# An attention and gated-MLP kernel on one core: another order of the first loads

## The chip, the cores and the metric

The kernel runs on one core of one Trainium2 chip. The metric is the time of one execution on the device in microseconds (us); lower is better. Five engines work side by side, each with its own queue of instructions: TensorE (PE, with weight loads shown as PEld), VectorE (DVE), ScalarE (ACT), GpSimd (POOL) and SyncE (SP), whose queue mostly issues transfers (DMA).

## The reference

One input x of 2048 rows and 640 columns (bf16) is normalised by rows and goes into two branches, whose results are added to x:

```
xn  = (x - mean(x)) / sqrt(var(x) + 1e-5)
qkv = xn @ wqkv                        # wqkv: 640 x 1920; 32 heads of 20
logits[s, w] = q[s] . k[s - 2w] * 20**-0.5     # w = 0..7; -1e9 where s - 2w < 0
o   = sum_w softmax(logits)[s, w] * v[s - 2w]
A   = o @ wo                           # 640 x 640
B   = ((xn @ w_gate) * (xn @ w_up)) @ w_down   # 640 x 1536, 640 x 1536, 1536 x 640
out = x + A + B
```

## The kernel before, in words

**Tiles.** The 2048 rows are 16 row tiles of 128 (a load is 128 x 640 bf16, 160 KB) and 4 blocks of 512 rows. The 640 columns are 5 chunks of 128 (`NCH`). A weight matrix lies in SBUF as chunks of 128 of its rows; `wqkv_load(g, lo, hi)` (L517) loads rows of chunks lo to hi of Q (g = 0), K (1) or V (2), 160 KB for each chunk. `x_load(t)` (L511) loads row tile t.

**Stages.** In the first stage (`front(t)`, L566, one for each row tile) VectorE takes the statistics of the tile in two halves (L574) and joins them (L577), ScalarE takes the root (L584), VectorE the reciprocal (L591) and, for tiles 0 to 5, the normalised rows (L603 in two parts for tiles 0 and 1, L606 for 2 to 5); from tile 6 on ScalarE normalises (L609) and the root is taken for two tiles at once. TensorE transposes tiles 0 to 3 (L642) and VectorE or ScalarE copies them from PSUM (L653, L655, L662); later tiles are transposed by DMA (L675). TensorE then projects Q and K: for tiles 0 and 1 by `spread` (L730), in two parts, chunks 0 to 1 and chunks 2 to 4, as the transposed rows come; for all others and for V by `mms` (L698). ScalarE evicts the projections (L703). Ahead of the first transposes TensorE runs ten dummy matmuls of 512 columns (`warm`, L682) and three of 256 behind them.

The second stage multiplies Q with shifted K on VectorE (L881, L930), sums some products on GpSimd (L956, L967, L989) and the heads' columns on TensorE (L1013: the logits); softmax follows on VectorE and ScalarE. In the third, VectorE multiplies V by the weights (L1192), GpSimd adds pairs (L1197) and TensorE sums the rest in four batches (L1251). The MLP's matmuls (L1315) and the output's (L1416, L1467) fill TensorE throughout.

**What sets the order.** The kernel is planned when it is built. `Sched` holds a clock for every engine and for the data path; each task names what it reads and writes, a priority and its PSUM banks. `run` (L235) takes for each engine, among the tasks that could start within a short patience, the one of the best priority, and emits the one that starts earliest. What an instruction costs in the plan is `occ`; a transfer ends in the plan when its bytes would have passed, or at `land` where that is given. The result is a fixed order for each engine with semaphore waits for the true dependences, so `land` and `occ` alone issue nothing, but they set the order.

The first loads are written out by hand (L1521 to L1529) and all go through SP's queue; `loads` (L521) goes on with tiles 3 to 11, then V's weights, then the last four tiles as their slots come free. Tile 1 starts its statistics only after tile 0 is normalised, and tile 2 after tile 1 (`have("apply", ...)`, L614 to L618). An instruction that waits holds up all behind it on its engine.

Of the kernel before, what the change touches and what calls it, by code (L numbers as in the profile page):

```python
# [11 lines left out]
NCH = 5  # L12
# [343 lines left out]
def build_kernel(nc, A_x, A_wqkv, A_wo, B_x, B_w_gate, B_w_up, B_w_down, out):  # L356
# [25 lines left out]
    NXS = 12  # L382
# [78 lines left out]
    def mark(*k):  # L461
        done.add(k)
# [4 lines left out]
    def have(*k):  # L467
        return lambda: k in done

    def num(n, *k):  # L470
        return lambda: count.get(k, 0) >= n
# [4 lines left out]
    def dma(o, i, r=(), w=(), name="", eng="sp", group=None, land=None):  # L476
        n = mybir.dt.size(o.dtype)
        for s in o.shape:
            n *= s
        return op(eng, lambda e: e.dma_start(o, i), r=r, w=w, dma=True, name=name, nbytes=n, group=group, land=land)  # L480
# [27 lines left out]
    def xslot(t):  # L508
        return t + 4 if t < 8 else t - 8

    def x_load(t, eng="sp", land=None):  # L511
        dma(XST[:, xslot(t), :], xhbm[t * TS:(t + 1) * TS, :], w=[XST[:, xslot(t), :]], name=f"xld{t}", eng=eng, land=land)
        mark("x", t)
# [3 lines left out]
    def wqkv_load(g, lo=0, hi=NCH, eng="sp", land=None):  # L517
        dst = WQKV[:, WPOS[g], lo:hi, :]
        dma(dst, wqkv_src[:, lo:hi, g * D:(g + 1) * D], w=[dst], name=f"ld_wqkv{g}_{lo}", eng=eng, land=land)

    def loads():  # L521
        def t(f, *a):
            return Task("sp", lambda: f(*a), prio=0)

        for t_ in range(3, NXS):
            yield t(x_load, t_)
        yield t(wqkv_load, 2)
        for t_ in range(NXS, NT):
            yield have("apply", t_ - NXS)
            yield t(x_load, t_)  # L530

        def w(T, src):
            dma(T[:], src.rearrange("(c p) n -> p c n", p=128), w=[T[:]], name="ld_w")

        def pads():
            z = ZERO[:, 0:PAD].unsqueeze(1).to_broadcast([128, NCH, PAD])
            dma(vscr[:, 0:PAD].rearrange("(c p) s -> p c s", p=128), z, r=[ZERO[:, 0:PAD]], w=[("vscr", "pad")], name="vpad")

        yield have("xnt", NT - 1)
        yield t(w, WG, B_w_gate)  # L540
        yield t(pads)
        yield t(w, WU, B_w_up)

        def copy_x():
            a, b = ohbm[0:3 * JB, :], xhbm[0:3 * JB, :]
            o, i = a.rearrange("(p r) n -> p (r n)", p=128), b.rearrange("(p r) n -> p (r n)", p=128)
            op("sp", lambda e: e.dma_start(o, i), w=[("outx",)], dma=True, name="outx", nbytes=2e6)

        yield num(2, "lg")
        yield t(copy_x)  # L550
# [15 lines left out]
    def front(t):  # L566
        x, st = XST[:, xslot(t), :], STATS[:, t, 0:12]
        xs, mv = XNS[:, t % NXN, :], MV[:, t, 0:2]
        sd, rstd, nmr = SD[:, t, 0:1], SD[:, t, 1:2], SD[:, t, 2:3]
# [9 lines left out]
        ts = next((g for g in GROUPS if t in g), (t,))  # L579
        t0, t1 = ts[0], ts[-1] + 1  # L580

        def sqrt():
            o, i = SD[:, t0:t1, 0:1], MV[:, t0:t1, 1:2]
            op("act", lambda e: e.activation(o, i, ACT.Sqrt, bias=EPSC[:, 0:1]), r=[("mv", k) for k in ts] + [EPSC[:]],  # L584
               w=[("sd", k) for k in ts], name=f"sd{t}", occ=0.25)
            for k in ts:
                mark("sd", k)

# [37 lines left out]
        if t == ts[-1]:  # L626
            yield Task("act", sqrt, r=[("mv", t)], prio=p - 1)
            yield Task("dve", recip, r=[("sd", t)], prio=p)
# [892 lines left out]
    x_load(0, land=3.2)  # L1521
    tch = A_wqkv.rearrange("(c k p) n -> k c p n", k=16, c=NCH)[:, :, 0, 0:32]
    stores.append(dma(TCH[0:16], tch, w=[TCH[0:16]], name="touch", eng="act"))
    wqkv_load(0, 0, 3, land=5.3)
    x_load(1, land=5.7)
    wqkv_load(0, 3, NCH, land=7.0)
    wqkv_load(1, 0, 3, land=8.5)
    x_load(2, land=9.0)
    wqkv_load(1, 3, NCH, land=10.0)  # L1529
    K.t["act"] = 2.1  # L1530
    warm(10, JB)

    def misc():
# [6 lines left out]
        yield Task("act", lambda: op("act", preload, name="exp_preload", occ=1.3), prio=6)  # L1540

    K.spawn(loads())
    for t in range(NT):
        K.spawn(front(t))
# [19 lines left out]
def bass_parallel_sum__sliding_local_dilated__glu_gated_bilinear__prompt_kernel(  # L1564
    nc, A_x, A_wqkv, A_wo, B_x, B_w_gate, B_w_up, B_w_down, out
):
    build_kernel(nc, A_x, A_wqkv, A_wo, B_x, B_w_gate, B_w_up, B_w_down, out)
# [28 lines left out]
```

## Time and profile before

| what | value |
|---|---|
| median of 3 runs | 265.47 us (265.27, 265.48, 265.47) |
| the profiled execution, its own time | 265.01 us |
| its span, first to last instruction | 263.3 us, 4080 instructions |
| granted clock of TensorE | 1.00 |
| VectorE busy | 218.9 us, 83% |
| ScalarE busy | 112.8 us, 43% |
| GpSimd busy | 160.6 us, 61% |

The profile is of one execution. Its pages give the busy time of each engine, the chain of work that ended last (followed back from the last instruction, at each step to what released it), groups of instructions by line, and for transfers the time from issue to landing. A line in a timeline is: start, length, engine, line, operation, tile written <- tile read, count, and in brackets the idle time before it with what ended it. Lengths of matmuls are modelled and overlap, so the pace of a row of matmuls is read from the starts of the first and of what follows. Transfers are named by the tile that they fill: XST is a row tile of x, WQKV weight rows.

### The profile page before, as it was taken

The numbers are of one execution on the slowest core, as the hardware profiler recorded it, in microseconds if no ns is written. First come the engines' busy times: TensorE is split into PE (matmuls) and PEld (weight loads), VectorE is DVE, ScalarE is ACT, GpSimd is POOL, SyncE is SP. The second block draws the span as 40 slices with busy tenths as digits, with TensorE's granted clock in tenths as the row PEclk, the third lists the DMA queues.
The fourth block names the chain that finished last, engine by engine and source line by source line (L and its number), as shares of the span: only waits on it lengthen the run. The fifth ranks groups of instructions, "written<-read, shape, count | busy, mean of one in ns | idle before, by whom it ended". The sixth has DMA issues, their size and how long they took to land.

```text
span 263.3 us, 4080 instructions
## 1 busy us (share of the span) xinstructions
PE 258.1 (98%) x1566; PEld 135.9 (52%) x1587; DVE 218.9 (83%) x259; ACT 112.8 (43%) x198; POOL 160.6 (61%) x97
## 2 busy tenths in 40 slices
PE   7999999999999999999999999999999999999996
PEld 3996965444444444444444444444444444445675
DVE  4687899999998798778779999999999989994041
ACT  3559987556612221224258656521350144211300
POOL 3000000000599998899973576799989999999100
PEclk9999999999999999999999999999999999999999
DMA  6964699970479996470249424847779676721621
GB/s 212 373 218 81 121 104 366 416 281 12 122 133 186 217 229 129 88 142 1 62 129 309 88 47 109 169 113 171 177 174 208 149 162 137 110 55 37 94 62 50
DMA packets 47843, 39.78 MB, mean 151 GB/s; under 512 B 23856, under 2 KB 45488, under 8 KB 47792
## 3 DMA queue, kind: packets, MB, share of 16 engines
q1 hardware_dynamic: 44848, 33.29, 49.5%
q0 software_dynamic: 2736, 6.16, 13.6%
q8 instruction: 12, 0.20, 0.3%
q10 hardware_dynamic: 240, 0.07, 0.1%
q14 instruction: 7, 0.06, 0.1%
HBM read 25.07 MB, written 7.23 MB: 123 GB/s over the span
## 4 chain that ended last, share of the span: by engine, by line
PE 91%; ACT 6%; issue 1%; DMA 1%; DVE 1%
PE PS L1315 39%; PE PS L1416 21%; PE PS L698 17%; PE PS L1467 7%; ACT XNS L609 3%; PE PS L730 2%; PE PS L1013 2%; PE PS L1251 2%; DMA XST<-in_A_x_dram 1%; ACT QT L703 1%; PE PS L642 1%; ACT VST L703 1%; ACT KT L703 1%; ACT SD L584 0%; DVE STATS L574 0%
## 5 line engine op out<-in xcount | busy, mean ns | idle before, releaser
L1197 POOL TENSOR_TENSOR SV<-PV 128x1024 bf16<-128x1024 f32 x40 | 94.2, 2522 | 15.7 <-DVE HT L1362 3.6
L1192 DVE TENSOR_TENSOR PV<-VX,PS 128x1024 f32<-128x1024 bf16 (+1 forms) x54 | 90.9, 1729 | 2.3 <-POOL SV L1197 2.3
L698 PE MATMUL PS<-XNT,WQKV 128*128 128x512 bf16 (+2 forms) x384 | 60.0, 316 | 0.5 <-issue 0.3
L1315 PE MATMUL PS<-XNT,WU 128*128 128x512 bf16 x239 | 59.4, 379 | 0.2 <-issue 0.2
L1315 PE MATMUL PS<-XNT,WG 128*128 128x512 bf16 x231 | 57.7, 379 | 0.6 <-ACT LOG L1024 0.2
L698 PEld LDWEIGHTS PS<-XNT,WQKV 128*128 128x128 bf16 x390 | 37.8, 112 | 21.9 <-ACT LOG L1024 0.8
L930 DVE TENSOR_TENSOR PRF<-PS,KT 128x1024 f32<-128x1024 f32 x32 | 37.9, 1217 | 0.3 <-PE PS L698 0.3
L1315 PEld LDWEIGHTS PS<-XNT,WU 128*128 128x128 bf16 x240 | 23.4, 98 | 28.5 <-ACT OT L1260 0.4
L1315 PEld LDWEIGHTS PS<-XNT,WG 128*128 128x128 bf16 x240 | 23.4, 98 | 28.5 <-issue 0.4
L956 POOL TENSOR_TENSOR PRF<-PRF,PRF 128x1024 f32<-128x1024 f32 x8 | 22.0, 2751 | 20.6 <-DVE LOG L1073 20.6
L703 ACT ACTIVATE HT<-PS 128x512 bf16<-128x512 f32 x24 | 14.3, 597 | 34.5 <-PE PS L1315 34.5
L881 DVE TENSOR_TENSOR PRD<-QT,KT 128x2048 bf16<-128x2048 bf16 x24 | 27.3, 1223 | 0.0
L1416 PE MATMUL PS<-HT,WD 128*128 128x512 bf16 x117 | 27.2, 380 | 0.1
L1032 POOL MEMSET LOG<- 32x6 bf16 (+6 forms) x7 | 0.4, 95 | 43.7 <-ACT LOG L1024 43.7
L703 ACT ACTIVATE UX<-PS 128x512 bf16<-128x512 f32 x15 | 9.0, 597 | 40.6 <-PE PS L1416 40.6
L989 POOL TENSOR_TENSOR PRD<-PRF,PRF 128x1024 bf16<-128x1024 f32 x8 | 21.4, 2759 | 0.1
L967 POOL TENSOR_TENSOR PRF<-PRF,PRD 128x1024 f32<-128x1024 f32 x8 | 19.5, 2544 | 0.0
L1416 PEld LDWEIGHTS PS<-HT,WD 128*128 128x128 bf16 x120 | 11.7, 98 | 14.3 <-ACT OT L1260 0.4
L1416 PE MATMUL PS<-OT,WO 128*128 128x512 bf16 x75 | 18.6, 379 | 0.1
L1480 DVE TENSOR_TENSOR FB<-PS,XR 128x320 bf16<-128x320 f32 (+2 forms) x9 | 4.1, 455 | 17.4 <-PE PS L1467 16.9
L1324 DVE TENSOR_TENSOR HT<-HT,PS 128x512 bf16<-128x512 bf16 x18 | 12.3, 684 | 7.0 <-PE PS L1315 7.0
L574 DVE BATCH_NORM_STATS2 STATS<-XST 128x6 f32<-128x320 bf16 x32 | 14.0, 470 | 2.4 <-DMA XST<-in_A_x_dram 2.4
(76 smaller groups left out, 246.4 us busy)
## 6 DMA issues: line engine op xcount, KB each, us to landing
VX<-v_scratch SPq DMA_DIRECT2D x80, 130.0 KB, 3.0
PRF<-PRF POOLq DMA_DIRECT2D x8, 512.0 KB, 5.1
XST<-in_A_x_dram SPq DMA_DIRECT2D x16, 160.0 KB, 5.3
v_scratch<-VST SPq DMA_DIRECT2D x4, 640.0 KB, 6.3
WG<-in_B_w_gate_dram SPq DMA_DIRECT2D x1, 1920.0 KB, 9.8
WU<-in_B_w_up_dram SPq DMA_DIRECT2D x1, 1920.0 KB, 14.0
out_dram<-in_A_x_dram SPq DMA_DIRECT2D x1, 1920.0 KB, 20.0
WD<-in_B_w_down_dram SPq DMA_DIRECT2D x1, 1920.0 KB, 8.1
```

Source lines behind the costliest of these rows:

```text
L698: op("pe", (lambda o, l, x, c, first: lambda e: e.matmul(o, l, x, start=first, stop=(c == NCH - 1)))(o, l, x, c, first), r=[l, x], w=[o], ...
L703: X = op("act", (lambda o, i: lambda e: e.activation(o, i, ACT.Copy))(o, i), r=[i], w=[o], name=name, occ=0.12 + n * 0.9e-3)
L881: op("dve", lambda e: e.tensor_tensor(s[:], qb, kv, ALU.mult), r=[q, rk], w=[s[:]], name=f"prod{j}_{r}_{c}", occ=1.15, lock=True)
L930: X = op("dve", lambda e: e.tensor_tensor(o[:], qb, kv, ALU.mult), r=[q, rk, ("qev", j, c)], w=[o[:]], name=f"prow{j}_{r}_{c}_{q0}", occ=1.17)
L956: yield Task("pool", lambda: op("pool", lambda e: e.tensor_tensor(x, x, y, ALU.add), r=[x, y] + tokens(), w=[x], name=name, occ=2.36, lock ...
L967: yield Task("pool", lambda: op("pool", lambda e: e.tensor_tensor(x, x, z, ALU.add), r=[x, z] + tokens(), w=[x], name=name + "c", occ=2.36 ...
L989: yield Task("pool", lambda: op("pool", lambda e: e.tensor_tensor(o, a, y, ALU.add), r=[a, y] + tokens(), w=[o], name=f"qend{j}_{r}_{q0}", ...
L1192: last[0] = op("dve", lambda e: e.tensor_tensor(p, vw, a, ALU.mult), r=[vv] + rk, w=[p], name=f"pv{u}_{x}_{r0}", occ=0.09 + 1.1 * nr)
L1197: X = op("pool", lambda e: e.tensor_tensor(o, p[:, :, 0, :], p[:, :, 1, :], ALU.add), r=[p[:]] + tokens(), w=[o], name=f"pva{u}_{x}", occ= ...
L1315: op("pe", (lambda l, x, c: lambda e: e.matmul(PS[:, b, :], l, x, start=(c == 0), stop=(c == NCH - 1)))(l, x, c), r=[l, x], w=[PS[:, b, :] ...
L1416: op("pe", (lambda l, x, i: lambda e: e.matmul(PS[:, b, :], l, x, start=(i == 0), stop=(i == n - 1)))(l, x, i), r=[l, x], w=[PS[:, b, :]], ...
L1467: op("pe", (lambda l, x, i: lambda e: e.matmul(dst, l, x, start=(i == 0), stop=(i == n - 1)))(l, x, i), r=[l, x], w=[PS[:, b, :]], name=f" ...
```

## The change

The loads written out by hand get another order and one more transfer. Before: tile 0, Q chunks 0-2, tile 1, Q 3-4, K 0-2, tile 2, K 3-4, and tile 3 from `loads`. After: tile 0, Q chunk 0, tile 1, Q 1-2, Q 3-4, tile 2, K 0-2, tile 3, K 3-4. The landing times given to the plan change with it, and so does the plan's cost of the root. Bytes, tiles and the work on every engine are the same; the order of work is planned anew from these numbers. Tile 0 is still loaded in one transfer, and there are ten dummy matmuls as before.

```diff
@@ loads
-        for t_ in range(3, NXS):
+        for t_ in range(4, NXS):
             yield t(x_load, t_)
@@ front / sqrt
-               w=[("sd", k) for k in ts], name=f"sd{t}", occ=0.25)
+               w=[("sd", k) for k in ts], name=f"sd{t}", occ=0.36)
@@ build_kernel
     x_load(0, land=3.2)
...
-    wqkv_load(0, 0, 3, land=5.3)
-    x_load(1, land=5.7)
-    wqkv_load(0, 3, NCH, land=7.0)
-    wqkv_load(1, 0, 3, land=8.5)
-    x_load(2, land=9.0)
-    wqkv_load(1, 3, NCH, land=10.0)
+    wqkv_load(0, 0, 1, land=4.0)
+    x_load(1, land=4.5)
+    wqkv_load(0, 1, 3, land=5.4)
+    wqkv_load(0, 3, NCH, land=6.3)
+    x_load(2, land=6.8)
+    wqkv_load(1, 0, 3, land=8.6)
+    x_load(3, land=9.0)
+    wqkv_load(1, 3, NCH, land=9.9)
     K.t["act"] = 2.1
     warm(10, JB)
```

## The prediction

> **What bounds the kernel now.** I read the busy totals first, then the chain of waits in order of time, then landings of the first transfers, then the waits of TensorE alone.
>
> ```profile
> PE 258.1 (98%) x1566; PEld 135.9 (52%) x1587; DVE 218.9 (83%) x259; ACT 112.8 (43%) x198; POOL 160.6 (61%) x97
> ```
>
> TensorE is busy 258.1 of 263.3 us. A busy share can hide waits, so the chain:
>
> ```profile
> 0.82 2.36 DMA XST<-in_A_x_dram
> ...
> 6.26 1.40 PE PS L730 x25
> ...
> 8.21 3.54 PE PS L730 x60
> ...
> 20.90 0.60 ACT VST L703
> ...
> 35.07 9.66 PE PS L698 x44
> ```
>
> Two readings. Up to 8.21 us TensorE waits for the first two row tiles (load, statistics on VectorE, root on ScalarE, normalising, transposes); from 8.21 it runs on. Between 20.9 and 35.07 the chain leaves TensorE for ScalarE, which would make ScalarE the limit there. The windows deny it:
>
> ```profile
> 25.00:30.00 5.00, 5.00 (x48) 5.00 (x47) 4.24 (x17) 5.00 (x10) 0.00 (x0) 1.00 0.63 125
> 30.00:35.00 5.00, 5.00 (x46) 4.97 (x46) 4.57 (x9) 5.00 (x11) 0.00 (x0) 1.00 0.99 127
> ```
>
> The columns are the length, then busy time and count for PE, PEld, DVE, ACT and POOL. TensorE and ScalarE are both full. TensorE's pace there is 10.00/94 = 0.106 us per 256-column matmul; a 128-column one takes 0.0565 (60 weight loads in 3.39 us from 8.20), a 512-column one 0.2158 (the 49 plus 0.05 us of the chain's 10.74 us pieces). From 14.26 to 44.73 stand 60, 110 and 70 of these: 3.39 + 11.66 + 15.11 = 30.16 of 30.47 us. So at most 0.31 us of waiting is in that whole stretch, although the chain runs through ScalarE: the two only tie. Later the chain is TensorE in pieces of 10.74 us to 261.0.
>
> Now the first transfers, by when they were issued and how long they took to land (160 KB is a row tile, 480 KB three weight rows, 320 KB two):
>
> ```profile
> WQKV<-in_A_wqkv_dram SPq DMA_DIRECT2D x1, 480.0 KB, 3.7
> XST<-in_A_x_dram SPq DMA_DIRECT2D x1, 160.0 KB, 3.7
> WQKV<-in_A_wqkv_dram SPq DMA_DIRECT2D x1, 320.0 KB, 4.0
> WQKV<-in_A_wqkv_dram SPq DMA_DIRECT2D x1, 480.0 KB, 5.4
> XST<-in_A_x_dram SPq DMA_DIRECT2D x1, 160.0 KB, 5.3
> WQKV<-in_A_wqkv_dram SPq DMA_DIRECT2D x1, 320.0 KB, 5.7
> ```
>
> Issues at 1.27, 1.73, 2.25, 2.75, 3.24 and 3.78 us (the timeline of the SP queue) give landings at 4.97 (Q rows 0-2), 5.43 (tile 1), 6.25 (Q rows 3-4), 8.15 (K rows 0-2), 8.54 (tile 2) and 9.48 (K rows 3-4). Tile 0 landed at 3.18, tile 3 (4.26 + 5.7) at 9.96. Against the bytes queued up to each (160, 640, 800, 1120, 1600, 1760, 2080, 2240 KB) the landings climb steadily, about 0.45 us per 160 KB, with one dent after 1120 KB. So a landing is set by the bytes ahead of it, and the order is what the change trades.
>
> **The change, part by part.**
>
> *New landings*, interpolated at the same byte counts: Q row 0 (320 KB) 3.8, tile 1 (480) 4.4, Q rows 1-2 (800) 5.43, Q rows 3-4 (1120) 6.25, tile 2 (1280) 6.9, K rows 0-2 (1760) 8.54, tile 3 (1920) 9.0, K rows 3-4 (2240) 9.96. Each against its consumer:
> - Tile 1: its statistics start at 5.45, right behind tile 0's normalising (4.90 + 0.64, with the usual 0.09 of overlap), 0.02 after it landed. Its spare grows from 0.02 to about 1 us; gain in this execution nothing. In an execution where it lands later, before pays and after doesn't.
> - Q rows 1-2: the first group now waits for a second transfer after five matmuls. They start at 6.05, so the sixth needs it at 6.33; it lands 5.43. Cost nothing. Behind that wait stand the rest of the group and tile 1's transposes (7.53).
> - Q rows 3-4: needed by the sixteenth at 6.05 + 15 x 0.0565 = 6.90, there at 6.25. Cost nothing, spare 0.65.
> - K rows 0-2: needed after 25 more at 9.62, there 8.54. K rows 3-4: at 8.21 + 40 x 0.0565 = 10.47, there 9.96. Nothing; spares 1.1 and 0.5 (1.5 and 1.0 before).
> - Tile 2: VectorE waited for it from 8.15 to 8.61; this 0.45 goes. TensorE then had 60 matmuls to do, so it isn't on the path.
> - Tile 3: its first statistic would start at 9.09, there 9.0.
>
> *One more issue on SP*, 0.45 us: SP's fourteen loads ended at 14.04 and it next issued at 17.48 after waiting for VectorE, so 3.4 us cover it; without that cover the first DMA transpose would come 0.45 later.
>
> *The planner's numbers* (landings, 0.36 for the root) issue nothing, but reorder everything behind. In the built program VectorE takes tile 3's first statistic (0.47) ahead of tile 2's reciprocal, in the 0.36 us in which it waited for the root; behind it stand tile 2's normalising and transposes. Statistics end 9.57, normalised at 10.25, wanted by TensorE at 8.21 + 50 x 0.0565 = 11.03 (50 now stand ahead of the transposes instead of 60): spare 0.8. Tile 3: transposes wanted at 11.03 + 0.28 + 25 x 0.0565 = 12.72; copying tile 2 ends at 12.0, reciprocal to normalised took 0.65 (13.04 to 13.69), so 12.65: spare 0.07, and a slip is paid one for one. ScalarE's root of tile 3 moves ahead of the first K eviction; it is done near 11.2, when that eviction becomes ready.
>
> *Further on* the same filling takes several waits of 0.36 to 0.70 us out of VectorE, and the normalising on ScalarE moves ahead of one or two V evictions of 0.5. I put the start of the products (31.66) about 1.1 us earlier, bounds 0 and 2.2. This buys nothing by itself, since TensorE is full. But TensorE's order uses it: the first logits stand ten 512-column matmuls earlier, 44.73 - 2.16 = 42.57. Their tenth product ended at 31.66 + 10 x 27.34/24 = 43.05; with 1.1 of lead 41.95, so no wait.
>
> *The later sums* (L1251, at 169.30, 194.34, 221.54, 246.08) move by 0, +1.08, -2.16 and -1.63 us (groups of five at 1.08; twelve 320-column matmuls at 4.89/36). GpSimd's tenth additions ended at 168.36, 193.21, 218.65 and 243.43, so even without a lead the spares are 0.9, 2.2, 0.7 and 1.0.
>
> *The sum.* Start 0 (bounds: 0 and +1.2, below); order of work 0 (-0.3, the waiting found above, to +0.6, a missed logits slot); tile 1's arrival 0 to -0.46 in ordinary runs. The profiled execution took 265.01, its span 263.3 and 1.7 around it; the median of the runs shown is 265.47, 0.46 above. I take -0.15 for tile 1's arrival against the median: **265.3 us**, which is no change: about 0.2% (0.53 us) is what a measurement of this kernel tells from none.
>
> *A rule against the change.* The Trainium skill, "DMA: Bandwidth & Descriptors", section "Bandwidth", says to batch transfers to 1 MiB, and its section on the anatomy of one DMA gives each (on the GpSimd path) a fixed 2.0 us. By that page, as an estimate, the split of the 480 KB load would cost 2 us, Q rows 1-2 would come at 7.4 and the time would be 1.1 us longer. The rows say otherwise: tile 1 landed 0.46 us behind the load ahead of it, so a completion lies beside the next transfer's data.
>
> **The rivals.**
> 1. *Slower, about 266.2: Q rows 3-4 come late.* The dent: the fifth transfer in the queue, issued 2.75, took 5.4 us, and data flow fell to 145 GB/s near 5.8 us. Before, the fifth was K rows 0-2, with 1.5 us to spare; now it is Q rows 3-4, with 0.65. If the delay belongs to the fifth place and not to its bytes, they land up to 2.75 + 5.4 = 8.15, 1.25 late; halfway is 0.7. Tile 1's transposes and all behind slip by it. It decides from 7.43. Against: 320 KB instead of 480, and the landings follow bytes.
> 2. *Slower, about 266.1: the first logits come too soon.* Without the lead of VectorE they wait 43.05 + 0.1 - 42.57 = 0.6 us. For: 0.07 us of spare at tile 3. Against: the 0.45 at tile 2 alone nearly covers it.
> 3. *Faster, about 264.8: the start was late in ordinary runs.* With tile 1 only 0.02 ahead of its reader in the best execution, the 0.46 of the median may be its lateness; that and 0.2 of the waiting in the projections go. Against: the runs agree within 0.2.
> 4. *Faster, about 264.3: ScalarE does bound 21 to 35 us*, as the chain has it, and its lead of 1.1 reaches the end. Against: the pace sum above.
> That the order of loads changes nothing in the program isn't possible: the built order differs on every engine.
>
> **How the numbers follow.** No change 0.42, rival 1 0.16, rival 2 0.12, rival 3 0.22, rival 4 0.08. Faster 0.30, same 0.42, slower 0.28. The forecast's own range is 264.94 to 266.0; to leave no more than 2 in 10 out I go from 264.4 (nearly rival 4) to 266.4 (rival 1 at 0.9).
>
> **What would show it.** Right: the second stretch of L730 matmuls starts at 8.2; the first wait of VectorE on tile 2 is gone; products start near 30.5; first logits near 42.6 without a wait; end of TensorE at 261. Rival 1 shows as a wait of TensorE inside the first 25 matmuls and a start after 8.3; rival 2 as a gap ahead of L1013; rivals 3 and 4 as a start before 8.2 or shorter stretches between 21 and 45. A wait of TensorE behind 60 us would make all of this wrong, and the range with it.

## The result, and the profile after

| | before | after |
|---|---|---|
| median | 265.37 us (265.12 to 266.11, 10 runs) | 266.44 us (266.07 to 267.29, 10 runs) |
| profiled execution, its own time | 265.01 us | 266.19 us |
| its span, instructions | 263.3 us, 4080 | 264.4 us, 4102 |

The ratio is 1.0044, with a 95% interval from 1.0029 to 1.0058: the change made the kernel 0.8 to 1.5 us slower. The forecast was 265.3, no change, and the time lies just beyond the slow end of its range (266.4).

From the page of the kernel after, the busy totals, and one of the costliest groups (busy time, mean ns of one, then the idle time ahead of it and what ended it):

```profile
PE 259.7 (98%) x1587; PEld 135.9 (51%) x1587; DVE 218.9 (83%) x259; ACT 112.6 (43%) x198; POOL 160.7 (61%) x97
L1315 PE MATMUL PS<-XNT,WG 128*128 128x512 bf16 x240 | 59.7, 379 | 0.6 <-DVE XNT L1324 0.6
```

TensorE is as full as it was, and 21 more of its matmuls are on record (1587, before 1566; some are missing from a trace), which alone can make the busy sum larger. So a busy share can't tell where the time went. The new entry is the 0.6 us of idle time ahead of one gate group. To place the loss, the same events are compared in both timelines. TensorE's last group of matmuls starts 1.16 later (before, then after):

```profile
260.56 0.44 PE L1467 MATMUL PS<-WO,OT 128*128 128x128 bf16 x5
```

```profile
261.72 0.44 PE L1467 MATMUL PS<-WO,OT 128*128 128x128 bf16 x5
```

The 1.16 has two parts:

- First sums (L1251): 169.69 instead of 169.23. 0.46 is lost ahead of them, all of it ahead of 13 us.
- From the first sums to the last group: 92.03 us instead of 91.33. 0.70 is lost behind them.

**The start.** The timeline of the kernel after:

```profile
6.19 1.80 PE L730 MATMUL PS<-XNT,WQKV 128*128 128x128 bf16 x25
7.23 0.60 PEld L730 LDWEIGHTS PS<-XNT,WQKV 128*128 128x128 bf16 x10 [0.20 <-DMA WQKV<-in_A_wqkv_dram]
8.48 3.14 PE L730 MATMUL PS<-XNT,WQKV 128*128 128x128 bf16 x50 [0.22 <-DVE XNT L653]
9.94 0.49 DVE L574 BATCH_NORM_STATS2 STATS<-XST 128x6 f32<-128x320 bf16 x1 [0.48 <-DMA XST<-in_A_x_dram]
11.46 0.44 PE L642 MATMUL PS<-IDENT,XNS 128*128 128x128 bf16 x5
```

The first 25 projections hold a wait of 0.20 for weight rows ahead of the last ten of them: those are Q rows 3 and 4. The second stretch starts at 8.48, not 8.21, and VectorE waits 0.48 for tile 3. The landings (issue, then us to landing) say why:

```profile
WQKV<-in_A_wqkv_dram SPq DMA_DIRECT2D x1, 160.0 KB, 2.4
XST<-in_A_x_dram SPq DMA_DIRECT2D x1, 160.0 KB, 3.4
WQKV<-in_A_wqkv_dram SPq DMA_DIRECT2D x1, 320.0 KB, 4.0
WQKV<-in_A_wqkv_dram SPq DMA_DIRECT2D x1, 320.0 KB, 4.5
WQKV<-in_A_wqkv_dram SPq DMA_DIRECT2D x1, 320.0 KB, 6.1
```

Issued at 1.27, 1.73, 2.20 and 2.68, the first four land at 3.7, 5.1, 6.2 and 7.2. Q row 0 is on time; tile 1, Q rows 1 and 2 and Q rows 3 and 4 come 0.7 to 0.95 behind the forecast by bytes (4.4, 5.43, 6.25). The last line is K rows 3 and 4, issued at 4.71: they land at 10.8, 0.85 behind the forecast (9.96).

The 8.48 accounts for 0.27 of the 0.46. Most of the rest lies in the 50 matmuls behind it: they take 2.98 (8.48 to 11.46) where the forecast's pace gives 50 x 0.0565 = 2.83. The last ten of them read K rows 3 and 4, and their first weight load starts at 10.87, right behind that landing.

How much of the 0.46 is the transfers' own? The profile of before is of one of its fastest runs (265.01). Experiment 5 below has the transfers of before as well, and its profile has:

```profile
8.55 3.55 PE L730 MATMUL PS<-XNT,WQKV 128*128 128x128 bf16 x60
169.57 1.26 PE L1251 MATMUL PS<-SV,SEL 128*32 128x512 bf16 x20
```

Its second stretch starts no earlier than in after, and its first sums only 0.12 earlier. So single profiles can't tell how much of the 0.46 is the transfers' and how much the spread of the start from run to run.

**The late part.** First the kernel before, around its first sums, then the kernel after (start, length, engine, line):

```profile
169.23 1.26 PE L1251 MATMUL PS<-SV,SEL 128*32 128x512 bf16 x20
169.71 2.56 ACT L1260 ACTIVATE OT<-PS 128x512 bf16<-128x512 f32 x5 [0.85 <-PE PS L1251]
170.43 2.76 PE L1416 MATMUL PS<-HT,WD 128*128 128x512 bf16 x12
170.80 0.68 DVE L1324 TENSOR_TENSOR XNT<-XNT,PS 128x512 bf16<-128x512 bf16 x1
```

```profile
168.79 0.68 DVE L1324 TENSOR_TENSOR XNT<-XNT,PS 128x512 bf16<-128x512 bf16 x1
169.38 0.42 DVE L1362 TENSOR_TENSOR XNT<-XNT,ZERO 128x512 bf16<-128x512 bf16 x1
169.69 1.26 PE L1251 MATMUL PS<-SV,SEL 128*32 128x512 bf16 x20
169.72 1.21 DVE L1192 TENSOR_TENSOR PV<-VX,PS 128x1024 f32<-128x1024 bf16 x1
170.16 2.56 ACT L1260 ACTIVATE OT<-PS 128x512 bf16<-128x512 f32 x5 [0.85 <-PE PS L1251]
170.85 0.68 DVE L1324 TENSOR_TENSOR XNT<-XNT,PS 128x512 bf16<-128x512 bf16 x1
171.59 1.25 PE L1315 MATMUL PS<-XNT,WG 128*128 128x512 bf16 x5 [0.64 <-DVE XNT L1324]
```

Behind the sums, before ran on with an output column (L1416) after 1.20 us; after waits 0.64 for a product of VectorE (L1324) and then runs a gate group (L1315). No data pass from that product to that group. What passes is a PSUM bank: the product (block 3, m=5) reads its up-projection from one, and the group is planned into it. The product itself is not late compared with before (170.85 against 170.80); VectorE is simply full. What moved is who needs its bank first. In the plan of before, by the planner's own clock, ScalarE's copy of the first sum ends at 170.10 and the product at 170.41, so the first group behind the sums got the copy's bank. In the new plan the two stand at 169.98 and 169.54: the order is swapped. On the chip the first of the five copies ends near 170.7 (170.16 and a fifth of 2.56) and the product at 171.53. The plan's figure for the product is 2 us too early in the new plan (1.1 in the old), and only the new plan leans on it.

**The lead of VectorE** came, and was lost. From the kernel after:

```profile
29.74 1.17 DVE L881 TENSOR_TENSOR PRD<-QT,KT 128x2048 bf16<-128x2048 bf16 x1
42.94 0.83 PE L1013 MATMUL PS<-PRD,G 128*32 128x512 bf16 x12
130.32 4.66 POOL L1197 TENSOR_TENSOR SV<-PV 128x1024 bf16<-128x1024 f32 x2
163.73 4.68 POOL L1197 TENSOR_TENSOR SV<-PV 128x1024 bf16<-128x1024 f32 x2 [2.08 <-DVE XNT L1362]
```

Products start at 29.74 (before 31.66), the first logits come at 42.94 without a wait, GpSimd's additions start at 130.32 (before 132.04). At 163.73 they stand where they stood in before:

```profile
163.69 4.67 POOL L1197 TENSOR_TENSOR SV<-PV 128x1024 bf16<-128x1024 f32 x2 [2.00 <-DVE PV L1192]
```

VectorE's queue holds products of the MLP, which wait for TensorE (11.0 us of its waits between 56 and 164 us end with a matmul of L1315, 10.6 in before), and so falls back to TensorE's pace.

### The profile page after: what moved, and what is told of

Same layout as the page of the kernel before. It is cut to its first block, busy times and chain, and to the rows that moved or that the text cites. A ratio compares the mean times of both kernels' runs of the same rounds, so it can differ in the third digit from the quotient of the medians.

```text
span 264.4 us, 4102 instructions
## 1 busy us (share of the span) xinstructions
PE 259.7 (98%) x1587; PEld 135.9 (51%) x1587; DVE 218.9 (83%) x259; ACT 112.6 (43%) x198; POOL 160.7 (61%) x97
## 4 chain that ended last, share of the span: by engine, by line
PE 92%; DVE 2%; DMA 2%; POOL 1%; issue 1%; SPq 1%; ACT 0%
PE PS L1315 36%; PE PS L698 23%; PE PS L1416 21%; PE PS L1467 7%; PE PS L1013 2%; PE PS L730 2%; DMA WQKV<-in_A_wqkv_dram 2%; DVE PV L1192 1%; PE PS L1251 1%; POOL SV L1197 1%; SPq L480 1%; DVE XNT L1324 1%; DVE XNT L1362 0%; PE PS L642 0%; ACT ZERO L703 0%
## 5 line engine op out<-in xcount | busy, mean ns | idle before, releaser
L1315 PE MATMUL PS<-XNT,WG 128*128 128x512 bf16 x240 | 59.7, 379 | 0.6 <-DVE XNT L1324 0.6
L1315 PE MATMUL PS<-XNT,WU 128*128 128x512 bf16 x240 | 59.6, 379 | 0.0
L1315 PEld LDWEIGHTS PS<-XNT,WG 128*128 128x128 bf16 x240 | 23.2, 98 | 29.6 <-DVE XNT L1324 1.6
L1315 PEld LDWEIGHTS PS<-XNT,WU 128*128 128x128 bf16 x240 | 23.5, 98 | 28.3
L956 POOL TENSOR_TENSOR PRF<-PRF,PRF 128x1024 f32<-128x1024 f32 x8 | 21.3, 2671 | 21.8 <-DVE LOG L1073 21.8
L1416 PE MATMUL PS<-HT,WD 128*128 128x512 bf16 x120 | 27.5, 379 | 0.0
L1416 PEld LDWEIGHTS PS<-HT,WD 128*128 128x128 bf16 x120 | 11.6, 98 | 14.4 <-ACT OT L1260 0.4
L1416 PE MATMUL PS<-OT,WO 128*128 128x512 bf16 x75 | 18.6, 379 | 0.0
L1324 DVE TENSOR_TENSOR HT<-HT,PS 128x512 bf16<-128x512 bf16 x18 | 12.3, 684 | 7.2 <-PE PS L1315 7.1
```

What stands on the lines that cost most here:

```text
L956: yield Task("pool", lambda: op("pool", lambda e: e.tensor_tensor(x, x, y, ALU.add), r=[x, y] + tokens(), w=[x], name=name, occ=2.36, lock ...
L1315: op("pe", (lambda l, x, c: lambda e: e.matmul(PS[:, b, :], l, x, start=(c == 0), stop=(c == NCH - 1)))(l, x, c), r=[l, x], w=[PS[:, b, :] ...
L1416: op("pe", (lambda l, x, i: lambda e: e.matmul(PS[:, b, :], l, x, start=(i == 0), stop=(i == n - 1)))(l, x, i), r=[l, x], w=[PS[:, b, :]], ...
```

## The experiments

Two theories. **A**: the order of work costs the time behind the sums, through that one bank. **S**: the transfers cost the time at the start. Each run is given as a ratio to the kernel before, timed beside it (its medians were 265.26 to 265.44), with a 95% interval.

**1. New transfers, old order of work.** The loads of after; the numbers given to the planner restore the order of before on PE, DVE, ACT and POOL. `K.t["sp"]` is the planner's clock for SyncE and `K.t_data` that for the data path, set behind the loads written by hand.

```diff
-               w=[("sd", k) for k in ts], name=f"sd{t}", occ=0.36)
+               w=[("sd", k) for k in ts], name=f"sd{t}", occ=0.25)
-    wqkv_load(0, 0, 1, land=4.0)
-    x_load(1, land=4.5)
...
+    wqkv_load(0, 0, 1, land=5.3)
+    x_load(1, land=5.7)
...
+    K.t["sp"], K.t_data = 4.64, 9.785
```

> The transfers of after, in its order, under the instruction order of before on the four compute engines. Theory A (the loss has two separate parts): only the start is paid. Q rows 3-4 land near 7.2 us, the second stretch of L730 matmuls starts near 8.5 instead of 8.2, K rows 3-4 cost another 0.1, and the time is 0.3 to 0.5 us above before: about 265.8. Rival B (all of the loss starts with the loads, the late wait is its echo): about 266.4. Rival C (all of it is the new order of work): 265.4, as before.

Measured 1.0008 [0.9999, 1.0017], 265.60. The wait behind the sums is gone (sums to last group 91.33 us). The transfers alone cost 0.2 us here, less than theory A's 0.3 to 0.5 and hardly told from nothing, so the time rules out rival B but not rival C. Its runs fall into two groups, six from 265.36 to 265.60 and five from 265.86 to 265.92.

**2. Old transfers, new order of work.**

```diff
-               w=[("sd", k) for k in ts], name=f"sd{t}", occ=0.25)
+               w=[("sd", k) for k in ts], name=f"sd{t}", occ=0.36)
-    wqkv_load(0, 0, 3, land=5.3)
-    x_load(1, land=5.7)
...
+    wqkv_load(0, 0, 3, land=5.4)
+    x_load(1, land=4.5)
...
+    K.t["sp"], K.t_data = 5.12, 9.1
```

> The transfers of before, under the instruction order of after on the four compute engines. Theory A: the start is that of before (second stretch near 8.2), and TensorE waits 0.6 to 1.1 us behind the first batch of sums for the bank that VectorE frees with the product of gate and up of the group before: 266.0 to 266.4. Rival B: no wait there, 265.4. Rival C: 266.4 with nothing lost at the start.

Measured 1.0029 [1.0018, 1.0040], 266.19: the order alone costs 0.8. Sums to last group 92.04. A second, smaller wait comes from the order meeting the old transfers: VectorE takes tile 3's statistic ahead of tile 2's reciprocal, tile 3 lands late, and TensorE waits 0.25 for tile 2's rows. In the timeline of this run:

```profile
10.57 0.49 DVE L574 BATCH_NORM_STATS2 STATS<-XST 128x6 f32<-128x320 bf16 x1 [0.23 <-DMA XST<-in_A_x_dram]
11.67 0.45 PE L642 MATMUL PS<-IDENT,XNS 128*128 128x128 bf16 x5 [0.25 <-DVE XNS L606]
```

**3. The gate group behind the output columns.** Is it the group's place?

```diff
+            if j == 3 and m == 6:
+                yield num(NCH, "dn", 0)
             hold = []
```

> After, with the one gate group that stands between the first batch of sums and the output matmuls put behind these, where before has it. Theory A: the wait of 0.64 us of TensorE behind the first batch of sums is gone and nothing takes its place: 0.7 below after, about 265.75; the start is still late (8.5). Rival D (the wait only moves on, to the output's matmuls or to the next sums): as after, 266.4.

Measured 1.0030 [1.0019, 1.0042], 266.23. The group moved, the wait stayed, now ahead of the first output column (L1326 and L1418 are L1324 and L1416 of the other kernels, two lines having been added above):

```profile
171.02 0.68 DVE L1326 TENSOR_TENSOR XNT<-XNT,PS 128x512 bf16<-128x512 bf16 x1
171.75 1.47 PE L1418 MATMUL PS<-HT,WD 128*128 128x512 bf16 x6 [0.63 <-DVE XNT L1326]
```

K rows 3 and 4, which land at 11.0 here, also cost TensorE a wait of 0.32 (at 11.05). So the place of the group was the wrong suspect. Whoever comes first is handed the bank that the plan believes free first.

**4. The planner is told that this bank comes free 3 us later.** One edit to the kernel after, and nothing else:

```diff
                     K.free_bank(hold[1], X)
+                    if j == 3 and m == 5:
+                        K.banks[hold[1]] += 3.0
```

> The changed kernel, but the planner is told that the PSUM bank of the product of block 3, m=5 comes free 3 us later than it reckons; it then hands the first output column the bank that ScalarE's copy of sum 0 frees, and the gate group of m=6 stands behind the output columns. Theory A (the late 0.64 us is the bank that VectorE's product behind its queue frees late, and nothing else): no wait of TensorE over 0.2 us between the first sums (about 169.7) and the first output matmul, TensorE's last end 0.6 to 0.7 earlier than in the changed kernel's profile (262.20), so about 261.55, time about 265.75 (265.5 to 266.0). Rival B (VectorE is late there anyway, and the late product only moves to the next one who needs it): a wait of 0.4 to 0.7 us turns up at the second to fifth output column or at gate group m=6, time 266.2 to 266.5.

Measured 1.0023 [1.0012, 1.0035], 265.81, against 1.0044 for after. From its timeline (L1418 is L1416, two lines further down):

```profile
169.72 1.26 PE L1251 MATMUL PS<-SV,SEL 128*32 128x512 bf16 x20
170.88 0.68 DVE L1324 TENSOR_TENSOR XNT<-XNT,PS 128x512 bf16<-128x512 bf16 x1
171.14 2.11 PE L1418 MATMUL PS<-HT,WD 128*128 128x512 bf16 x9 [0.16 <-issue]
...
221.40 1.03 PE L1315 MATMUL PS<-XNT,WG 128*128 128x512 bf16 x4 [0.34 <-DVE XNT L1324]
```

With the product as late as ever (170.88), TensorE goes on at 171.14 instead of 171.59. That is theory A. The profiles carry it more than the times do, whose intervals overlap a little (1.0012 to 1.0035, and 1.0029 to 1.0058). The cleanest pair is experiments 3 and 4: their plans put the instructions of PE, DVE, ACT and POOL in the same order, and only the banks differ. From the first sums to the last group experiment 3 takes 92.02 us, experiment 4 91.51; the times (1.0030 and 1.0023) go the same way, by less. A little of rival B is there too: behind the third sums the same kind of group waits 0.34 for the product of m=10. In after this cost nothing, since TensorE came there 0.7 later. Sums to last group: 91.51, so 0.52 of the 0.70 is recovered and 0.18 comes back.

This profile also shows which late transfer sets the start. Q rows 3 and 4 land at 7.0 and cause no listed wait, yet K rows 3 and 4 (issued at 4.72, 6.1 to landing: 10.8) are waited for:

```profile
10.90 0.60 PEld L730 LDWEIGHTS PS<-XNT,WQKV 128*128 128x128 bf16 x10 [0.28 <-DMA WQKV<-in_A_wqkv_dram]
```

In the four kernels with the transfers of after (after, 1, 3, 4) these rows land at 10.8 to 11.0, and the weight loads that read them start at 10.87, 10.82, 11.05 and 10.90, whatever came before. With the transfers of before they start at 10.42 in before and at 10.65 and 10.76 in experiments 2 and 5. So in after the 0.20 waited for Q rows 3 and 4 had no price of its own: without it TensorE would have waited longer at 10.87.

**5. Only the cost of the root**, with the transfers of before. It makes the planner put the same group on the same kind of bank:

```diff
-               w=[("sd", k) for k in ts], name=f"sd{t}", occ=0.25)
+               w=[("sd", k) for k in ts], name=f"sd{t}", occ=0.36)
```

> The kernel before with the one planner figure for ScalarE's square root raised from 0.25 to 0.36, all transfers as before. Its plan also puts the gate group m=6 directly behind the first sums, on the bank that the product of m=5 frees. Theory A (the bank sets it): a wait of 0.5 to 0.7 us behind the first sums at about 170.4, start as before, time 266.0 (265.8 to 266.3). Rival C (the early transfers set nearly all of the loss): 265.4, within 0.2 of before.

Measured 1.0025 [1.0017, 1.0034], 266.00, as theory A has it: one planner figure, changed by 0.11 us, costs 0.7. The wait in its timeline:

```profile
170.72 0.68 DVE L1324 TENSOR_TENSOR XNT<-XNT,PS 128x512 bf16<-128x512 bf16 x1
171.68 1.03 PE L1315 MATMUL PS<-XNT,WG 128*128 128x512 bf16 x4 [0.85 <-DVE XNT L1324]
```

Now the transfers, one property at a time, all with the order of work of before (runs 6 to 9 and 11; tile 3 is listed by hand in these, at its old place in 6, 9 and 11, and `K.t` and `K.t_data` are set as in run 1).

**6. Only the split of Q rows 0 to 2 (1 + 2 rows)**, tile 1 behind both:

```diff
-    wqkv_load(0, 0, 3, land=5.3)
+    wqkv_load(0, 0, 1, land=5.3)
+    wqkv_load(0, 1, 3, land=5.3)
```

> Before, with the first load of three Q rows cut into one row and two rows, in place, all other transfers in the order of before, instruction order of before. If one more transfer at the head of the queue is what delays all behind it (theory A, about 0.9 us for each landing after it): Q rows 3-4 land near 7.1, the second stretch starts near 8.5, time 0.2 to 0.5 above before. If the order of the bytes is what counts (rival E): Q rows 3-4 land near 6.3, start near 8.2, time as before, 265.4.

Measured 1.0022 [1.0013, 1.0032], 266.16. Q rows 3 and 4, fifth in the queue, are issued near 2.7, take 5.4 us and land at 8.1:

```profile
8.12 0.75 PE L730 MATMUL PS<-XNT,WQKV 128*128 128x128 bf16 x10 [0.83 <-DMA WQKV<-in_A_wqkv_dram]
```

**7. Tiles 2 and 3 one place ahead, no split.** The first four transfers are those of before.

```diff
     wqkv_load(0, 3, NCH, land=7.0)
-    wqkv_load(1, 0, 3, land=8.5)
     x_load(2, land=9.0)
+    wqkv_load(1, 0, 3, land=8.5)
+    x_load(3, land=10.585)
     wqkv_load(1, 3, NCH, land=10.0)
```

> The kernel before with tiles 2 and 3 each put one transfer ahead (tile 2 ahead of K rows 0 to 2, tile 3 ahead of K rows 3 and 4), the first four transfers as before, the order of work as before. Theory S (what costs at the start is a transfer in fifth or later place that TensorE needs soon): Q rows 3 and 4 keep the fourth place and land at about 6.6, so nothing waits there; K rows 0 to 2 in sixth place land at about 9.4 to 9.7 and K rows 3 and 4 at about 10.8 to 11.0, so 0 to 0.4 us between 9.6 and 11; time 265.4 to 265.8. Rival T (the order of the loads is worth nothing, only their number counts): 265.4, and no wait.

Measured 0.9999 [0.9990, 1.0007], 265.40: this part of the change is worth nothing either way. K rows land at 8.5 and 9.8, a microsecond ahead of theory S, and no wait of TensorE names a transfer. It does wait 0.22 for tile 1's normalised rows, behind tile 1, which lands at 5.8 here (5.43 in the profile of before).

**8. Tile 1 ahead of Q rows 0 to 2**, no split, tiles 2 and 3 ahead as in 7:

```diff
-    wqkv_load(0, 0, 3, land=5.3)
     x_load(1, land=5.7)
+    wqkv_load(0, 0, 3, land=5.3)
```

> The kernel before with tile 1 ahead of Q rows 0 to 2 and tiles 2 and 3 each one transfer ahead, no split, the order of work as before. Theory S: Q rows 0 to 2 in third place land at 5.6 to 5.9, and TensorE, which needed them at about 5.1, starts the products 0.4 to 0.8 us later while dummies and transposes hold it; time 265.7 to 266.2. Rival T (dummies and transposes would have held TensorE till then at a low pace anyway): 265.3 to 265.5.

Measured 1.0025 [1.0007, 1.0042], 265.76. Q rows 0 to 2 land at 1.73 + 5.0 = 6.73, and the first projections start at 6.85, in the profile of before at 6.10. The time is the one that theory S gave; the landing is 0.8 us or more later than it said. Ten of the runs lie between 265.40 and 266.11 and two near 267.6, which nothing here explains.

**9. The split elsewhere:** Q rows 3 and 4 as two transfers, in fourth and fifth place. If fifth place makes a transfer late, the last row must be late.

```diff
-    wqkv_load(0, 3, NCH, land=7.0)
+    wqkv_load(0, 3, 4, land=7.0)
+    wqkv_load(0, 4, NCH, land=7.0)
```

> The kernel before with the other Q load split, and one transfer more in the queue: tile 0, Q rows 0 to 2 (480 KB, in one), tile 1, Q row 3, Q row 4, then K as before; order of work as before. Theory P (place: the transfer that comes fifth lands 0.9 us or more later than it did in fourth place, as in the split of Q rows 0 to 2 alone): the last Q row lands at 7.2 to 8.0, TensorE waits 0.2 to 0.8 us in its first 25 products, time 265.6 to 266.2. Theory Z (size of the second transfer: with 480 KB in second place 1.20 to 1.28 MB had come by 6 us, with 160 KB there 1.05 to 1.15 MB, in ten profiles; it is the small second transfer that leaves the flow low at 3 to 4 us): 1.2 MB or more by 6 us, the last Q row lands at about 6.5 to 6.7, no wait over 0.1 us, time within 0.2 of before (265.3 to 265.5).

Measured 0.9996 [0.9987, 1.0005], 265.28. The last Q row lands at 6.5, TensorE doesn't wait. Place is ruled out. What moved is the flow; the transfers' view of the first 6 us, for this run and, below it, for before and after:

```profile
DMA packets 1183, 1.30 MB, mean 216 GB/s; under 512 B 175, under 2 KB 1183, under 8 KB 1183
```

```profile
DMA packets 1116, 1.23 MB, mean 205 GB/s; under 512 B 160, under 2 KB 1116, under 8 KB 1116
```

```profile
DMA packets 1003, 1.08 MB, mean 180 GB/s; under 512 B 164, under 2 KB 1003, under 8 KB 1003
```

**10. Q row 0 on ScalarE's queue**, in the kernel after with its bank told later:

```diff
-    wqkv_load(0, 0, 1, land=4.0)
+    wqkv_load(0, 0, 1, eng="act", land=4.0)
```

> The changed kernel with the bank told later, and Q row 0 issued by ScalarE, so that SyncE's queue holds tile 0, tile 1, Q rows 1 and 2, Q rows 3 and 4 with one issue less ahead of each. Theory I (the issue of about 0.47 us for each transfer is what makes the later ones late): Q rows 3 and 4 are issued at 2.2 and land at 6.3 to 6.7, no wait in TensorE's first 25 products, time 0.2 to 0.4 less than with the bank told later alone (ratio 1.0023): 265.4 to 265.6 against a before of 265.3. Theory Z (what counts is the large second transfer): the flow by 6 us stays at 1.05 to 1.15 MB, Q rows 3 and 4 land at about 7, time as with the bank told later alone, 265.7 to 265.9.

Measured 1.0007 [0.9998, 1.0016], 265.43, against 1.0023 for experiment 4. Q rows 3 and 4 are issued at 2.2 and land at 6.3; nothing waits for them. Issue theory I has it by the time. But the flow rose too, which neither theory had said:

```profile
DMA packets 1159, 1.26 MB, mean 210 GB/s; under 512 B 179, under 2 KB 1159, under 8 KB 1159
```

The landing moved by 0.5 to 0.9 (6.8 to 7.2 in the four profiles with the transfers of after) for an issue moved by 0.48. K rows 3 and 4 land at 10.1, and nothing waits for them either. The Trainium skill, "Trainium Kernel Development and Optimization", section "Key Constraints", holds that transfers issued from several engines run on the same 16 DMA engines, and that several issuers only save issue time. In this one profile the landing gained that much or up to twice as much.

**11. The split 2 + 1** instead of 1 + 2 in experiment 6: is it how much is queued by 1.7 us?

```diff
-    wqkv_load(0, 0, 1, land=5.3)
-    wqkv_load(0, 1, 3, land=5.3)
+    wqkv_load(0, 0, 2, land=5.3)
+    wqkv_load(0, 2, 3, land=5.3)
```

> As the split of Q rows 0 to 2 alone (1 + 2 rows, which took ratio 1.0022 and waited 0.83 us for Q rows 3 and 4), but split 2 + 1: tile 0, Q rows 0 and 1 (320 KB), Q row 2, tile 1, Q rows 3 and 4. Number of transfers, places, bytes ahead of each later one and the order of work are the same; only the second transfer is 320 instead of 160 KB. By the issue timelines SyncE takes about 0.46 us for each issue, so 480 KB instead of 320 KB are queued by 1.7 us. Theory J (where 320 KB or less are queued by 1.7 us the flow drops: 1.05 to 1.15 MB by 6 us and 1.58 to 1.82 by 8; with 480 KB or more 1.20 to 1.30 and 1.89 to 2.01): 1.2 MB or more by 6 us, Q rows 3 and 4 land at 6.7 to 7.0, TensorE waits less than 0.2 us, time within 0.2 of before. Theory Z2 (it takes a whole 480 KB transfer in second place, or a second queue): 1.05 to 1.15 MB by 6 us, a wait of 0.4 to 0.9 us, ratio 1.0015 to 1.003.

Measured 1.0029 [1.0019, 1.0038], 266.15, 1.07 MB by 6 us, and Q rows 3 and 4 at 8.4. Theory J falls:

```profile
8.44 0.75 PE L730 MATMUL PS<-XNT,WQKV 128*128 128x128 bf16 x10 [1.19 <-DMA WQKV<-in_A_wqkv_dram]
```

All profiles together:

| the transfer behind tile 0 in SyncE's queue | kernels | MB by 6 us | MB by 8 us |
|---|---|---|---|
| 480 KB in one | before, experiments 2, 5, 7, 9, 12 | 1.20 to 1.30 | 1.89 to 2.01 |
| 160 or 320 KB | after, experiments 1, 3, 4, 6, 8, 11 | 1.07 to 1.15 | 1.58 to 1.82 |
| 160 KB, with 160 KB on ScalarE's queue beside it | experiment 10 | 1.26 | 1.89 |

The two groups don't overlap. Why the flow drops isn't settled. Place is ruled out, and so is theory J's limit: 480 KB were queued by 1.7 us in experiment 11, and the flow was low. All kernels of the first row had 640 KB queued by then, so in one queue a limit between 480 and 640 KB isn't told from the size of the second transfer. A queue of its own for one small transfer helps: experiment 10 had 480 KB queued by 1.7 us, and the flow was high.

**12. Both costs taken away:** the order of work of experiment 4 with the transfers of experiment 7. It is also the only trial of whether VectorE's lead is worth something.

```diff
     x_load(0, land=3.2)
...
-    wqkv_load(0, 0, 1, land=4.0)
-    x_load(1, land=4.5)
-    wqkv_load(0, 1, 3, land=5.4)
+    wqkv_load(0, 0, 3, land=5.4)
+    x_load(1, land=4.5)
     wqkv_load(0, 3, NCH, land=6.3)
...
+    K.t["sp"], K.t_data = 5.12, 9.1
```

> The changed kernel's order of work with the bank told later, and the transfers with tiles 2 and 3 one place ahead but no split (Q rows 0 to 2 in one, in second place). It takes both costs away and keeps VectorE's lead. If the bank and the small second transfer are all of the loss: about as before, 265.2 to 265.5, 1.2 MB or more by 6 us. If VectorE's lead is worth something once neither cost stands: 264.6 to 265.1. If the order of work holds a further cost: 265.6 or more.

Measured 1.0007 [0.9998, 1.0016], 265.46. The loss is gone and nothing is won. K rows 3 and 4 land at 10.0 and aren't waited for. Sums to last group 91.51: the 0.18 behind the third sums is in it again.

| ratio to before | order of before | order of after | of after, bank told later |
|---|---|---|---|
| transfers of before | 1 | 1.0029 | not run |
| transfers of after | 1.0008 | 1.0044 | 1.0023 |
| tiles 2 and 3 ahead, no split | 0.9999 | not run | 1.0007 |

The order costs 0.8 to 1.0 us by this table (1.0029 to 1; 1.0044 to 1.0008), where the profiles show 0.70; the transfers cost 0.2 to 0.4 (1.0008 to 1; 1.0044 to 1.0029; 1.0023 to 1.0007). The intervals, about 0.001 to each side, cover that disagreement, and by the times alone the cost of the transfers is barely told from none. No version ran faster than before: experiment 9 has the lowest median, 265.28 beside 265.33, which is no difference.

## Why the prediction was wrong

- **"A landing is set by the bytes ahead of it", start 0.** Wrong. Landings were read off a curve whose transfers all followed a 480 KB one. With a small transfer there, 0.08 to 0.16 MB less than in before arrives in 6 us. The term of the start, 0, measured 0.46 between the two profiles and 0.2 to 0.4 in the table above. Part of the 0.46 is chance, since that profile of before was one of its fastest runs (265.01): against experiment 5 it is 0.12.
- **Spares by consumer.** The times of need were right or nearly so (Q rows 3 and 4 needed at 6.90 in the forecast; TensorE stood there near 7.0), the landings weren't. The spare that failed is that of K rows 3 and 4: "there 9.96", 0.5 ahead of 10.47. They landed at 10.8 to 11.0, and TensorE read them right behind that, at 10.82 to 11.05, in all four kernels with these transfers. Tile 3, given no spare, was late by 0.48 on VectorE, without a wait of TensorE; the 0.22 ahead of 8.48 is a wait for tile 1's transposed rows, behind the late ones.
- **Rival 1, Q rows 3 and 4 late in fifth place.** The wait came where it said, but it didn't set the price: 0.20 was waited against 0.7 to 1.25, and K rows 3 and 4 would have taken as much without it. Its reason was wrong: experiment 9 has a fifth transfer in time. In experiments 6 and 11 its full price was paid (0.83 and 1.19), with tile 1 behind the split; that the change put tile 1 ahead of Q rows 1 and 2 goes with the smaller wait, but no pair of runs isolates it.
- **"Order of work 0", with +0.6 for a missed logits slot.** The upper bound was the right size by luck, and the place was wrong. The logits came without a wait (rival 2 wrong); a bank of VectorE's product behind the first sums cost 0.64 instead. The forecast checked those sums for when their inputs are ready (spare 0.9) and never for which bank the next group gets. It named a wait of TensorE behind 60 us as what would make it wrong, and there was one.
- **VectorE's lead buys nothing.** Right, and tested: experiment 12 keeps it, has neither of the two costs but the 0.18 behind the third sums, and stands at 1.0007.
- **Tile 1's lateness in ordinary runs, -0.15 (rival 3).** The lateness is real: in experiment 7 tile 1 comes third, as in before, VectorE waits 0.25 for it, the second stretch starts at 8.57, and the profiled run took 265.37. Both figures are 0.36 above those of before's profile. The gain didn't come, since after waits for K rows 3 and 4 instead. Whether it would come with those in time stays open: in experiment 10 tile 1 landed at 4.3 and the second stretch starts at 8.36, but 0.2 is lost again behind the third sums (91.54), and the ratio is 1.0007.
- **ScalarE as the bound (rival 4).** It needed a gain from the lead, and none came.
- **One more issue on SyncE's queue: 0.** In itself yes (experiment 9 has the same number of issues as after).
- **The rule on batching** that the forecast set aside (the Trainium skill, "DMA: Bandwidth & Descriptors", section "Bandwidth", and the fixed 2.0 us of "Anatomy of one DMA — SWDGE (gpsimd) path", given there for transfers that GpSimd issues). By the forecast's estimate from it, Q rows 1 and 2 were to land at 7.4. They landed at 6.2, so 2 us aren't added for one more transfer in SyncE's queue. The direction of the rule was right where the split falls on the second transfer (1.0022), and wrong where it falls on the fourth (0.9996).

## What to carry to other kernels

When a planner is fed new numbers, compare not only the order of instructions but who gets whose buffer: look at each place where a full engine takes a PSUM bank that a busy engine releases, and measure the plan's release times against the trace. A plan's error of 1 to 2 us costs nothing until a changed number makes the plan lean on it. And a landing time read from one order of transfers doesn't carry over to another by counting bytes: in these runs a large transfer directly behind the first served best, and a split behind that cost nothing. Look also past the first late transfer: a later one can set the price.

## What the runs showed of the hardware

- How much data had come by 6 us went with the second transfer in the queue: 1.20 to 1.30 MB with one of 480 KB, 1.07 to 1.15 with a smaller one, in thirteen profiles; a second queue for one small transfer gave 1.26.
- The first 160 KB transfer took 2.3 to 2.6 us from issue to landing in all profiles.
- The same 320 KB (Q rows 3 and 4) took from 4.0 to 5.7 us from issue to landing, depending on how the transfers ahead of them were cut.
- The ten dummy matmuls took 3.88 to 4.43 us at a granted clock of 1.00 in all profiles, without a relation to what the kernel loads: 3.94 in before, 3.88 in after, 4.42 or 4.43 in experiments 1, 2, 3, 5, 6, 8 and 9. When they are slow, the 0.5 us wait for the normalised tile 0 is shorter or gone, and the time is hardly moved (265.25 in the profiled run of experiment 9).
